# A long convolution with a gated block on Trainium2: the last phase's matmuls in plain float32 instead of high and low halves

## The chip, the cores and the metric

The kernel runs on one core of a Trainium2 chip. A core has five engines that run side by side, each through its own queue of instructions in order: TensorE (PE; its weight loads are shown as PEld), VectorE (DVE), ScalarE (ACT), GpSimd (POOL) and SyncE (SP), which here only issues transfers. Matmul results land in PSUM, everything else lies in SBUF, and transfers between SBUF and the chip's memory (DMA) are issued from SyncE's and ScalarE's queues. The metric is the time of one execution on the device in microseconds, as the median over several runs.

## The reference

All arrays are float32, with B = 4 batches, S = 12800 positions and D = 128 channels. A filter is made by a small network from a position table and multiplied with a decaying window. The product x * v is convolved causally with that filter for each channel, written with transforms of length 2S, and multiplied with x. The result goes through a gated block: a causal depthwise convolution of 5 taps and a sigmoid make the gate, a matrix makes the value, and a second matrix the output.

```python
def _attn_ref(x, v, pos_emb, w1, w2):
    h_filt = (np.maximum(pos_emb @ w1, 0.0) @ w2) * window      # [S, D]
    u = x * v
    L = 2 * S
    Uf = np.fft.rfft(u, n=L, axis=1)
    Hf = np.fft.rfft(h_filt, n=L, axis=0)
    y = np.fft.irfft(Uf * Hf[None, :, :], n=L, axis=1)[:, :S, :]
    return x * y

def _moe_ref(x, w_val, conv_w, w_out):                          # x: the result above
    gate_pre = sum(conv_w[k] * xp[:, k:k + S, :] for k in range(5))   # xp: x with 4 zeros ahead
    gate = 1.0 / (1.0 + np.exp(-gate_pre))
    return gate * (x @ w_val) @ w_out
```

## The kernel before

The sequence is cut in two blocks (index `j`) of 6400 = 100 x 64 positions, and a transform of 6400 points is done in two stages, over 100 and over 64. The kernel has three phases.

The first makes the filter and the first stage of the spectra of x * v and stores them in the chip's memory (`a_u`). The second goes over 100 frequencies: second stage, products with the filter, the inverse's first stage, stored in `c_y`. Both stay as they are, but for one thing: in the first phase the constant matrix `inv` is split in halves (L148 and L149 in the helper `split`), with the result kept for the last phase.

"Split" means that a float32 value a is written as hi + lo, both in the type float32r, where hi is a rounded to that type and lo = a - hi. A product a * b then becomes three matmuls, hi*hi, lo*hi and hi*lo, summed in PSUM.

The third phase goes over 8 units, one for each batch and block. For a unit two generators run:

- `conv_out` does the inverse's second stage and the multiplication with x. It goes over 8 chunks of 8 rows (n2), each of 100 x 2 x 1024 values from `c_y`. `prep` issues the chunk's loads two chunks ahead (x for two chunks at L431, or L434 in the last unit; c_y at L438), then makes the halves: `hi` by ScalarE (L444) and `lo` by GpSimd (L447), each in two pieces of 100 x 1024. In the first 11 chunks one of the two `lo` pieces goes to VectorE. A chunk has two groups of 4 rows. A group is six matmuls into `y_ps` (L412), a multiplication with x on VectorE (`at`, L413), four transposes on TensorE (`tp`, L394) and a copy by ScalarE into `ext` (L396), which holds the unit's result with channels on partitions.
- `gated_out` does the gated block for the unit before, in 5 pieces of 1280 positions: the gate's first tap on ScalarE (L455), four more taps on VectorE (L462, two inputs from SBUF), the sigmoid on ScalarE (L464); the value product in parts of 512, 512 and 256 columns into `v_ps`. The first part is split: `vh` on ScalarE (L489), `vl` on GpSimd (L490), three matmuls (L492); the other two parts are plain float32 (L494). VectorE multiplies with the gate (`gd`, L495), TensorE multiplies with the output matrix (`o_ps`, L506), ScalarE copies (`o_sb`, L507) and issues the store (L513).

`mix` interleaves the two generators' steps in the program's order. The first unit's `conv_out` runs alone, since no gated block is ready. The last unit is laid out by rows, and its gated block (`gated_rows`, L459 and L526 to L540) starts before its `conv_out` is done; its value products are plain float32 already. One tap of it is added by GpSimd (L459).

The order on each engine is not exactly the order of the program: a planner arranges the instructions with its own estimate of their durations before the kernel is built, keeps dependencies, and sets the waits. Buffers limit how far things run ahead: six load buffers `ld` shared by x and c_y loads (an x buffer is free after the second chunk's `at`, a c_y buffer after the last instruction that reads it), two of `y_ps`, `v_ps`, `tp3` and `o_ps` in PSUM, two of `hi`, `lo`, `vh` and `vl`. SyncE's queue holds the x and c_y loads in one order, so that a load that waits for a buffer holds up those behind it.

Of the kernel before, what the change touches and what calls it, by code (L numbers as in the profile page):

```python
# [9 lines left out]
F32 = mybir.dt.float32  # L10
F32R = mybir.dt.float32r
I32 = mybir.dt.int32
AF = mybir.ActivationFunctionType
ALU = mybir.AluOpType
PSUM = bass.MemoryType.PSUM
DRAM = bass.MemoryType.DRAM

# The causal convolution of length S = 2 * M is cut in two blocks of M = N1 * N2 samples,
# n = n1 * N2 + n2. A block's polynomial is evaluated at the M roots of z^M = i,
# k = k1 + N1 * k2, in two stages (over n1, then over n2 with the twiddles in the matrix).  # L20
# With z^M = i a product of two real blocks comes back as (low half) + i (high half), so
#   y0 = Re inv(H0 U0),   y1 = Re inv(H0 U1 + (H1 - i H0) U0)
# and no block is padded.
B, S, D, FO, KC = 4, 12800, 128, 64, 5
J, N1, N2 = 2, 100, 64
M = N1 * N2
KG = 8
P1C = 2
CH = 8
# [27 lines left out]
def _narrow(nc, pool, dst, src):  # L57
    """dst (float32) = src, whose 64-bit words are doubles, rounded to nearest."""
    p, n = dst.shape
    raw = pool.tile([p, n], mybir.dt.int64, name="raw")  # L60
    nc.scalar.dma_start(out=raw, in_=src)
    words = raw.bitcast(I32).rearrange("p (n w) -> p n w", w=2)
    lo, hi = words[:, :, 0], words[:, :, 1]
    ve = nc.vector
    top = pool.tile([p, n], I32, name="top")
    tmp = pool.tile([p, n], I32, name="tmp")
    ve.tensor_scalar(out=top, in0=hi, scalar1=0x07FFFFFF, scalar2=3, op0=ALU.bitwise_and, op1=ALU.logical_shift_left)
    ve.tensor_single_scalar(out=tmp, in_=hi, scalar=-0x40000000, op=ALU.bitwise_and)
    ve.tensor_tensor(out=top, in0=top, in1=tmp, op=ALU.bitwise_or)
    ve.tensor_single_scalar(out=tmp, in_=lo, scalar=29, op=ALU.logical_shift_right)  # L70
    ve.tensor_tensor(out=top, in0=top, in1=tmp, op=ALU.bitwise_or)
    # the 29 bits below, in units of the value's own power of two
    ve.tensor_single_scalar(out=tmp, in_=lo, scalar=0x1FFFFFFF, op=ALU.bitwise_and)
    rest = pool.tile([p, n], F32, name="rest")
    ve.tensor_copy(out=rest, in_=tmp)
    ve.tensor_single_scalar(out=tmp, in_=top, scalar=-0x00800000, op=ALU.bitwise_and)
    ve.scalar_tensor_tensor(rest, rest, 2.0 ** -52, tmp.bitcast(F32), op0=ALU.mult, op1=ALU.mult)
    ve.tensor_tensor(out=rest, in0=rest, in1=top.bitcast(F32), op=ALU.add)
    # below float32's range: zero
    ve.tensor_scalar(out=tmp, in0=hi, scalar1=27, scalar2=15, op0=ALU.logical_shift_right, op1=ALU.bitwise_and)  # L80
    keep = pool.tile([p, n], F32, name="keep")
    ve.tensor_single_scalar(out=keep, in_=tmp, scalar=7, op=ALU.is_ge)
    ve.tensor_tensor(out=dst, in0=rest, in1=keep, op=ALU.mult)
# [3 lines left out]
def tile_longconv_gate(  # L87
# [19 lines left out]
    nc = tc.nc  # L107
# [3 lines left out]

    # spectra after the first stage: [k1][re|im][n2][block][...][d]
    a_u = dram.tile([N1, 2, N2, J, B, D], F32, name="a_u")
    # products after the inverse's first stage: [block][batch][k1][re|im, n2][d]
    c_y = dram.tile([J, B, N1, 2 * N2, D], F32, name="c_y")
# [37 lines left out]

    # the filter's channels before w2, after the first stage: [re|im, n2][k1][block][channel]
    ag_pool = tc.tile_pool(name="ag", bufs=1)
    ag = ag_pool.__enter__().tile([128, N1, J, FO], F32, name="ag")

# [1 line left out]
    with tc.tile_pool(name="p1", bufs=1) as p1, tc.tile_pool(name="ps1", bufs=1, space=PSUM) as ps1:  # L159
# [4 lines left out]
        def filt():  # L164
            HC = 16
            for c0 in range(0, N2, HC):
# [3 lines left out]
                for j in range(J):  # L170
                    for n in range(0, HC, 8):
# [17 lines left out]
                        yield  # L189
            # block 1 holds H1 - i H0  # L190
            E = 4
            for j in range(J):
                for e0 in range(0, FO, E):
# [10 lines left out]
                    yield  # L204
            # the second stage, in place: [block, channel][k1][re|im, k2]
            for k0 in range(0, N1, 4):
# [35 lines left out]

        inv_split = []

        def signal():
            ready = [prep(0)]
            for i, (j, n0) in enumerate(chunks):
                if i == 8:
                    inv_split.extend(split(inv, "inv"))
                    _narrow(nc, p1, wval, w_val)  # L250
                    _narrow(nc, p1, wout, w_out)
                    _narrow(nc, p1, cw, conv_w.rearrange("k d -> d k"))
# [22 lines left out]

        # the filter's steps are spread over the signal's by their time on the tensor engine
        FS = 0.9
# [13 lines left out]

# [1 line left out]
    with tc.tile_pool(name="p2", bufs=1) as p2, tc.tile_pool(name="ps2", bufs=1, space=PSUM) as ps2:  # L293
# [3 lines left out]
        def tail(k1, g_l, z_ps, h_sb):  # L297
# [7 lines left out]

            # [V0 | H0 U1 | H1' U0], then the last two added
            v_t = p2.tile([128, J + 1, BD], F32, name="v_t2", bufs=4)
# [65 lines left out]
    ag_pool.__exit__(None, None, None)  # L373
    inv_hi, inv_lo = inv_split

# [1 line left out]
    with tc.tile_pool(name="p3", bufs=1) as p3, tc.tile_pool(name="ps3", bufs=1, space=PSUM) as ps3:  # L377
        xv = x.rearrange("b (j a n) d -> b j a n d", j=J, a=N1)
        HALO = KC - 1
        ROW_STEPS = 40  # L380
        wval_hi, wval_lo = split(wval, "wval")

        def conv_out(b, j, ext, rows=None):
            """y of one block, times x, transposed: ext[d, HALO + token]; with rows, a list
            for the chunks that are done, ext[d, HALO + n2, n1] and the last chunk first"""
            if rows is None:
# [14 lines left out]
            for q in order(b, j):  # L401
                hi, lo, xt = preps.pop(0)
                if todo:
                    preps.append(prep(*todo.pop(0)))
                at = p3.tile([N1, CH, D], F32, name="at", bufs=2)
                for g in range(CH // G):
                    y_ps = ps3.tile([N1, G, D], F32, name="y_ps", bufs=2)
                    gs = slice(g * G, (g + 1) * G)
                    es = slice(g * G * D, (g + 1) * G * D)
                    ops = [(w, d, c) for w, d in ((inv_hi, hi), (inv_lo, hi), (inv_hi, lo)) for c in range(2)]  # L410
                    for i, (w, d, c) in enumerate(ops):
                        nc.tensor.matmul(out=y_ps, lhsT=w[:, c], rhs=d[:, c, es], start=(i == 0), stop=(i == len(ops) - 1))  # L412
                    nc.vector.tensor_tensor(at[:, gs], y_ps, xt[:, gs], op=ALU.mult)  # L413
# [10 lines left out]
        def prep(b, j, q):  # L424
            ns = slice(q * CH, (q + 1) * CH)
            i = order(b, j).index(q)
            if i % 2 == 0:
# [11 lines left out]
                out=ct, in_=c_y[j, b].rearrange("k (c n) d -> k c n d", c=2)[:, :, ns].rearrange("k c n d -> k c (n d)"))  # L439
            hi = p3.tile([N1, 2, CH * D], F32R, name="hi", bufs=2)  # L440
            lo = p3.tile([N1, 2, CH * D], F32R, name="lo", bufs=2)
            for h in range(2):
                hs = slice(h * CH * D // 2, (h + 1) * CH * D // 2)
                nc.scalar.copy(out=hi[:, :, hs], in_=ct[:, :, hs])  # L444
                # until the gates run, the vector engine has room for half of this
                eng = nc.vector if h == 0 and (b * J + j) * (N2 // CH) + q < 11 else nc.gpsimd
                eng.tensor_tensor(lo[:, :, hs], ct[:, :, hs], hi[:, :, hs].bitcast(F32), op=ALU.subtract)  # L447
            return hi, lo, xt

        def gate(ext, t0, W=TCH, shift=1, pooled=0):  # L450
            """the gate's elementwise chain, an instruction at a time; pooled: taps added by GpSimd"""
            sl = lambda k: ext[:, t0 + k * shift:t0 + k * shift + W]
# [14 lines left out]
        def gated_out(b, j, ext):  # L467
# [4 lines left out]
            for t0 in range(0, M, TCH):  # L472
# [9 lines left out]
                for e in range(0, TCH, 512):  # L482
                    w = min(512, TCH - e)
                    v_ps = ps3.tile([D, 512], F32, name="v_ps", bufs=2)
                    part = ext[:, HALO + t0 + e:HALO + t0 + e + w]
                    if e == 0:
                        vh = p3.tile([D, 512], F32R, name="vh", bufs=2)
                        vl = p3.tile([D, 512], F32R, name="vl", bufs=2)
                        nc.scalar.copy(out=vh, in_=part)  # L489
                        nc.gpsimd.tensor_tensor(vl, part, vh.bitcast(F32), op=ALU.subtract)  # L490
                        for i, (a, d) in enumerate(((wval_hi, vh), (wval_lo, vh), (wval_hi, vl))):
                            nc.tensor.matmul(out=v_ps, lhsT=a, rhs=d, start=(i == 0), stop=(i == 2))  # L492
                    else:
                        nc.tensor.matmul(out=v_ps[:, :w], lhsT=wval, rhs=part, start=True, stop=True)  # L494
                    nc.vector.tensor_tensor(gd[:, e:e + w], v_ps[:, :w], sg[:, e:e + w], op=ALU.mult)  # L495
# [19 lines left out]
        def gated_rows(b, j, ext, rows):  # L515
            """the same by rows of N1 tokens, each chunk as soon as conv_out has it"""
            W = CH * N1
# [59 lines left out]

        # the last block goes by rows, so that its gate does not wait for all of it
        b, j = units[-1]
# [49 lines left out]
```

## Time and profile before

| | |
|---|---|
| median of 3 runs | 1739.79 us (1730.27 to 1749.66) |
| span of the profiled execution | 1744.1 us |
| mean granted TensorE clock | 0.887 |
| busy over the span: PE, DVE, ACT, POOL | 77%, 81%, 59%, 67% |
| share of the chain that ended last: DVE, DMA, issue, PE | 43%, 21%, 15%, 15% |
| first phase, second phase, last phase | to about 460 us, to about 1100 us, to the end |

The profile is of one execution; the span is its time from the first to the last instruction, and its share outside the span is not shown. "PEclk" is the part of TensorE's full clock that was granted. A row of instructions reads: line in the kernel, engine, operation, the tile written <- the tiles read, the shapes, xcount; then in a grouped view the busy time, the mean duration of one in nanoseconds, and the engine's idle time before them with what ended it; in the view in order of time, the row begins with its start and its length in microseconds and ends with the idle time before it in brackets. Matmul durations overlap, since matmuls are pipelined, and a matmul's cost in a stream is read from one start to the next. In the table of stretches, each engine has its busy time in that stretch and the number of instructions, and the last three columns are the granted clock, the share of the transfer engines' time and their rate.

### The profile page before, as it was taken

To read this page: it belongs to the slowest core of one execution; us is meant where nothing else is said; L and a number is where in the kernel's file an instruction comes from. 1 tells how busy PE (TensorE), PEld (TensorE's weight loads), DVE (VectorE), ACT (ScalarE), POOL (GpSimd) and SP (SyncE) were. 2 spreads that over 40 slices of the span, in tenths; PEclk is the share of its full clock that TensorE was granted. 3 is DMA by queue.
4 is the path that set the end of the run, shared out by engine and by line. 5 is a ranking of instruction groups with operands and counts; after the bars stand their busy time and mean duration, and the time that the engine had idled before them with its cause. 6 is when DMAs were issued, how large, how long until landed. Compare 5 with 4: busy or idle time off the path is not lost.

```text
span 1744.1 us, 16766 instructions
## 1 busy us (share of the span) xinstructions
PE 1344.8 (77%) x5313; PEld 873.4 (50%) x5313; DVE 1418.7 (81%) x1204; ACT 1032.3 (59%) x1657; POOL 1168.2 (67%) x528
## 2 busy tenths in 40 slices
PE   4679988767677777677777676588888888889896
PEld 3567766544323333233333232356766676667675
DVE  5663337653399999999999999269999999999996
ACT  2235446552477777677777775255656565556765
POOL 2223333333299988878888888159978697788752
PEclk9798997885799989998999999687988998888899
DMA  6666666666656656555656553565555455555512
GB/s 227 243 243 241 246 236 234 241 235 253 220 203 198 212 181 205 179 177 181 203 178 211 173 185 99 170 216 168 183 191 158 159 183 161 172 177 166 177 61 91
DMA packets 224831, 332.97 MB, mean 191 GB/s; under 512 B 7832, under 2 KB 162500, under 8 KB 220108
## 3 DMA queue, kind: packets, MB, share of 16 engines
q1 hardware_dynamic: 99358, 226.12, 38.8%
q10 hardware_dynamic: 125386, 105.79, 18.3%
q8 instruction: 43, 0.70, 0.2%
q14 instruction: 44, 0.36, 0.1%
HBM read 200.80 MB, written 131.07 MB: 190 GB/s over the span
## 4 chain that ended last, share of the span: by engine, by line
DVE 43%; DMA 21%; issue 15%; PE 15%; ACT 3%; POOL 2%; SPq 1%; ACTq 0%; POOLq 0%; DVEq 0%
DVE gt L462 16%; DMA a_u<-st 13%; DVE v_t L316 9%; DVE v_t L317 5%; PE fp L264 4%; DMA ld<-c_y 4%; DVE v_t L311 3%; DVE v_t L312 3%; DMA ld<-in_x_dram 3%; DVE at L413 2%; PE o_ps L506 2%; DVE gd L495 2%; PE y_ps L412 2%; PE z_ps L367 1%; PE c_ps L326 1%
## 5 line engine op out<-in xcount | busy, mean ns | idle before, releaser
L447 POOL TENSOR_TENSOR lo<-ld,hi 100x1024 fp32r<-100x1024 f32 x117 | 373.0, 3209 | 116.9 <-ACT hi L444 115.2
L462 DVE SCALAR_TENSOR_TENSOR gt<-ext,cw,gt 128x1280 f32<-128x1280 f32 (+1 forms) x164 | 411.5, 2521 | 10.2 <-POOL gt L459 5.3
L238 POOL TENSOR_TENSOR u_lo<-u_t,u_hi 100x1024 fp32r<-100x1024 f32 x64 | 154.2, 2411 | 302.3 <-ACT u_hi L237 263.5
L367 PE MATMUL z_ps<-ld 128*128 128x512 f32 x400 | 215.7, 666 | 117.3 <-DVE v_t L312 97.7
L311 POOL TENSOR_TENSOR q_t<-zsw,h_sb 128x1024 f32<-128x1024 f32 x100 | 241.6, 2416 | 90.2 <-ACT zsw L300 90.2
L316 DVE TENSOR_TENSOR v_t<-v_t,q_t 128x1536 f32<-128x1536 f32 x100 | 277.6, 2806 | 1.2 <-POOL q_t L312 1.2
L326 PE MATMUL c_ps<-v_t,ld 128*128 128x512 f32 x400 | 208.0, 639 | 57.2 <-POOL v_t L320 29.1
L312 POOL TENSOR_TENSOR q_t<-zsw,h_sb 128x512 f32<-128x512 f32 x100 | 225.8, 2258 | 0.0
L364 ACT COPY h_sb<-h_ps 64x256 f32<-64x256 f32 x400 | 147.1, 368 | 103.0 <-DVE v_t L312 66.7
L264 PE MATMUL fp<-u_hi,fwd_hi 100*100 100x512 f32 x256 | 127.6, 499 | 90.3 <-ACT st L267 59.3
L269 DVE COPY st<-fp 100x512 f32<-100x512 f32 x128 | 84.6, 687 | 127.9 <-DMA a_u<-st 100.0
L367 PEld LDWEIGHTS z_ps<-ld 128*128 128x128 f32 x400 | 76.6, 206 | 205.8 <-issue 166.9
L506 PEld LDWEIGHTS o_ps<-wout,gd 128*128 128x128 f32 x700 | 167.9, 320 | 11.9 <-issue 2.5
L317 DVE TENSOR_TENSOR v_t<-v_t 128x448 f32<-128x448 f32 x100 | 172.6, 1757 | 0.1
L444 ACT CAST hi<-ld 100x1024 fp32r<-100x1024 f32 x128 | 128.0, 1048 | 71.1 <-DMA ld<-c_y 44.5
L326 PEld LDWEIGHTS c_ps<-v_t,ld 128*128 128x128 f32 x400 | 77.9, 205 | 179.2 <-issue 123.3
L506 PE MATMUL o_ps<-wout,gd 128*128 128x128 f32 x700 | 164.2, 384 | 0.7 <-DVE gd L495 0.7
L299 ACT ACTIVATE zsw<-z_ps 64x1024 f32<-64x1024 f32 x100 | 102.2, 1022 | 61.1 <-PE z_ps L367 56.9
L311 DVE TENSOR_TENSOR v_t<-z_ps,h_sb 128x1024 f32<-128x1024 f32 x100 | 121.1, 1211 | 18.5 <-ACT zsw L300 18.5
L267 ACT COPY st<-fp 100x512 f32<-100x512 f32 x128 | 69.7, 591 | 110.7 <-DMA a_u<-st 85.6
L237 ACT CAST u_hi<-u_t 100x1024 fp32r<-100x1024 f32 x64 | 68.0, 1064 | 107.1 <-PE fp L264 51.6
L236 DVE TENSOR_TENSOR u_t<-ld 100x1024 f32<-100x1024 f32 x64 | 82.5, 1290 | 57.0 <-POOL u_lo L238 49.9
(93 smaller groups left out, 2696.8 us busy)
## 6 DMA issues: line engine op xcount, KB each, us to landing
c_y<-c_sb ACTq DMA_DIRECT2D x100, 512.0 KB
ld<-c_y SPq DMA_DIRECT2D x64, 800.0 KB
ld<-a_u SPq DMA_DIRECT2D x49, 1024.0 KB
ld<-in_x_dram SPq DMA_DIRECT2D x66, 400.0 KB
ld<-in_v_dram SPq DMA_DIRECT2D x64, 400.0 KB
a_u<-st ACTq DMA_DIRECT2D x64, 400.0 KB
a_u<-st SPq DMA_DIRECT2D x64, 400.0 KB
ld<-in_x_dram SPq DMA_DIRECT2D x31, 800.0 KB
```

The source lines that it names most:

```text
L238: nc.gpsimd.tensor_tensor(lo, u_t, hi.bitcast(F32), op=ALU.subtract)
L264: nc.tensor.matmul(out=fp, lhsT=w[:, c], rhs=d[:, b:b + 2], start=(k == 0), stop=(k == 2))
L311: eng.tensor_tensor(fl(t[:, 0:J]), fl(z), h_b(c, 0, J * B), op=ALU.mult)
L312: eng.tensor_tensor(fl(t[:, J:J + 1]), fl(z[:, 0:1]), h_b(c, 1, B), op=ALU.mult)
L316: nc.vector.tensor_tensor(v_t, v_t, q_t, op=ALU.add)
L317: nc.vector.tensor_tensor(v_t[:, 1, CUT:], v_t[:, 1, CUT:], v_t[:, 2, CUT:], op=ALU.add)
L326: nc.tensor.matmul(out=c_ps, lhsT=g_l, rhs=v_t[:, j], start=True, stop=True)
L364: nc.scalar.copy(out=h_sb[half * N2:(half + 1) * N2, c], in_=h_ps[c * N2:(c + 1) * N2])
L367: nc.tensor.matmul(out=z_ps[:, j], lhsT=f_l, rhs=au[:, j], start=True, stop=True)
L447: eng.tensor_tensor(lo[:, :, hs], ct[:, :, hs], hi[:, :, hs].bitcast(F32), op=ALU.subtract)
L462: nc.vector.scalar_tensor_tensor(gt, sl(k), cw[:, k:k + 1], gt, op0=ALU.mult, op1=ALU.add)
L506: nc.tensor.matmul(out=o_ps[:, i], lhsT=gv[:, g0 + i], rhs=wout, start=True, stop=True)
```

## The change

The last phase no longer uses halves. The split of `inv` in the first phase and of `wval` at the start of the last go. `prep` returns the loaded chunk `ct` itself, without `hi` and `lo`, so the loaded chunk is now read by the matmuls. A group in `conv_out` has two plain float32 matmuls into `y_ps` (one for each of the two halves, real and imaginary) instead of six split ones. The first part of the value product is one plain float32 matmul like the other two, instead of a cast, a subtraction and three split matmuls. The rest of the diff takes away comments, with the line numbers kept.

```diff
-        inv_split = []
-
         def signal():
             ready = [prep(0)]
             for i, (j, n0) in enumerate(chunks):
                 if i == 8:
-                    inv_split.extend(split(inv, "inv"))
                     _narrow(nc, p1, wval, w_val)
...
-    inv_hi, inv_lo = inv_split
...
-        wval_hi, wval_lo = split(wval, "wval")
...
             for q in order(b, j):
-                hi, lo, xt = preps.pop(0)
+                ct, xt = preps.pop(0)
...
-                    ops = [(w, d, c) for w, d in ((inv_hi, hi), (inv_lo, hi), (inv_hi, lo)) for c in range(2)]
-                    for i, (w, d, c) in enumerate(ops):
-                        nc.tensor.matmul(out=y_ps, lhsT=w[:, c], rhs=d[:, c, es], start=(i == 0), stop=(i == len(ops) - 1))
+                    for c in range(2):
+                        nc.tensor.matmul(out=y_ps, lhsT=inv[:, c], rhs=ct[:, c, es], start=(c == 0), stop=(c == 1))
                     nc.vector.tensor_tensor(at[:, gs], y_ps, xt[:, gs], op=ALU.mult)
...
-            hi = p3.tile([N1, 2, CH * D], F32R, name="hi", bufs=2)
-            lo = p3.tile([N1, 2, CH * D], F32R, name="lo", bufs=2)
-            for h in range(2):
-                hs = slice(h * CH * D // 2, (h + 1) * CH * D // 2)
-                nc.scalar.copy(out=hi[:, :, hs], in_=ct[:, :, hs])
-                eng = nc.vector if h == 0 and (b * J + j) * (N2 // CH) + q < 11 else nc.gpsimd
-                eng.tensor_tensor(lo[:, :, hs], ct[:, :, hs], hi[:, :, hs].bitcast(F32), op=ALU.subtract)
-            return hi, lo, xt
+            return ct, xt
...
-                    if e == 0:
-                        vh = p3.tile([D, 512], F32R, name="vh", bufs=2)
-                        vl = p3.tile([D, 512], F32R, name="vl", bufs=2)
-                        nc.scalar.copy(out=vh, in_=part)
-                        nc.gpsimd.tensor_tensor(vl, part, vh.bitcast(F32), op=ALU.subtract)
-                        for i, (a, d) in enumerate(((wval_hi, vh), (wval_lo, vh), (wval_hi, vl))):
-                            nc.tensor.matmul(out=v_ps, lhsT=a, rhs=d, start=(i == 0), stop=(i == 2))
-                    else:
-                        nc.tensor.matmul(out=v_ps[:, :w], lhsT=wval, rhs=part, start=True, stop=True)
+                    nc.tensor.matmul(out=v_ps[:, :w], lhsT=wval, rhs=part, start=True, stop=True)
```

## The prediction

> **What bounds the kernel now.** I read the busy shares by stretch first, cut at the last `at` multiply of each unit (a unit is one block of one batch: 8 chunks, 16 groups of four rows). The last phase starts at 1106 us. The first fence is that table for the first unit, the start of the second, one steady unit, two others and the tail, then two `at` rows that mark the cuts.
>
> ```profile
> core 0: us, PE busy (x) PEld busy (x) DVE busy (x) ACT busy (x) POOL busy (x), PEclk, DMA share, GB/s
> 1106.00:1160.00 54.00, 37.52 (x156) 24.39 (x156) 19.25 (x23) 21.83 (x30) 19.52 (x8) 0.80 0.63 211
> 1160.00:1200.00 40.00, 31.65 (x105) 20.41 (x106) 37.00 (x27) 26.94 (x35) 36.97 (x12) 0.65 0.54 176
> 1228.00:1304.00 76.00, 65.12 (x289) 52.54 (x289) 73.61 (x54) 43.86 (x61) 64.31 (x23) 0.90 0.59 186
> 1384.30:1460.60 76.30, 64.72 (x298) 52.23 (x297) 73.03 (x54) 44.85 (x63) 65.03 (x21) 0.89 0.54 172
> 1460.60:1537.10 76.50, 64.55 (x295) 52.15 (x294) 74.09 (x53) 45.40 (x63) 60.15 (x22) 0.89 0.51 164
> 1685.10:1744.10 59.00, 43.73 (x222) 34.62 (x220) 41.01 (x47) 33.93 (x48) 15.81 (x7) 0.90 0.28 89
> ...
> 1227.34 0.68 DVE L413 TENSOR_TENSOR at<-y_ps,ld 100x512 f32<-100x512 f32 x1
> 1684.46 0.68 DVE L413 TENSOR_TENSOR at<-y_ps,ld 100x512 f32<-100x512 f32 x1
> ```
>
> From 1228.0 to 1685.1 are six units: 457.1 / 6 = 76.2 us each. In each, VectorE is busy 73 to 74 us. It looks like the bound, but its instructions are stretched. The next fence gives minimum, median and maximum of three lines between 1190 and 1640 us, and the longest wait of TensorE there.
>
> ```profile
> L462 DVE SCALAR_TENSOR_TENSOR gt<-ext,cw,gt x118: 1534/2738/6090, 1190.6 to 1636.2; 128x1280 f32<-128x1280 f32 x118
> L447 POOL TENSOR_TENSOR lo<-ld,hi x97: 2353/3607/4079, 1189.2 to 1638.6; 100x1024 fp32r<-100x1024 f32 x97
> L490 POOL TENSOR_TENSOR vl<-ext,vh x30: 1271/2532/2552, 1202.3 to 1636.2; 128x512 fp32r<-128x512 f32 x30
> PE tp L394 <- DVE at L413: 47.6, 21, 5.3
> ```
>
> The same tap of the gate (L462) takes 1.53 us or 6.09 us. GpSimd's subtractions spread likewise, 2.35 to 4.08 and 1.27 to 2.55. Add the minima as if no two of these ran at once: 20 taps x 1.53 + 16 `lo` x 2.35 + 5 `vl` x 1.27 = 30.6 + 37.6 + 6.4 = 74.6 us, against a unit of 76.2. So the unit behaves as if taps and subtractions took turns on something that I call the port, and TensorE waits behind that for `at`.
>
> **The change, part by part.** (1) Removed: all 16 `lo` and 5 `vl` subtractions per unit, the `hi` and `vh` casts on ScalarE, and 11 `lo` on VectorE in the first units. VectorE's work that stays:
>
> ```profile
> L447 DVE TENSOR_TENSOR lo<-ld,hi 100x1024 fp32r<-100x1024 f32 x11 | 15.1, 1375 | 32.9 <-ACT hi L444 32.9
> L413 DVE TENSOR_TENSOR at<-y_ps,ld 100x512 f32<-100x512 f32 x128 | 85.8, 680 | 15.4 <-PE y_ps L412 15.4
> L495 DVE TENSOR_TENSOR gd<-v_ps,sg 128x512 f32<-128x512 f32 x70 | 46.8, 679 | 8.8 <-PE v_ps L494 8.2 <-ACT sg L464 0.7
> L495 DVE TENSOR_TENSOR gd<-v_ps,sg 128x256 f32<-128x256 f32 x35 | 14.4, 411 | 0.5 <-PE v_ps L494 0.5
> L444 ACT CAST hi<-ld 100x1024 fp32r<-100x1024 f32 x128 | 128.0, 1048 | 71.1 <-DMA ld<-c_y 44.5 <-PE y_ps L412 22.5 <-POOL lo L447 3.9
> L149 DVE TENSOR_TENSOR inv_lo<-inv,inv_hi 100x200 fp32r<-100x200 f32 x1 | 0.4, 368 | 0.0
> ```
>
> Per unit: 20 x 1.53 + 16 x 0.68 + 10 x 0.68 + 5 x 0.41 = 50.3 us. ScalarE loses 16 x 1.05 = 17 us of its 45, and had room anyway. Neither can bound. The splits of the two weight matrices (`inv_lo`, 0.4 us, is the longest of four such instructions) lie early in the first phase: nothing.
>
> (2) TensorE. The fence has full-clock stretches; a cost is the distance from one start to the next.
>
> ```profile
> 1396.82 1.02 PE L494 MATMUL v_ps<-ext,wval 128*128 128x512 f32 x2
> 1397.68 0.51 PE L394 MATMUL tp<-ident,at 100*128 100x100 f32 x4
> ...
> 1400.34 0.60 PE L494 MATMUL v_ps<-ext,wval 128*128 128x256 f32 x2
> 1400.78 1.42 PE L506 MATMUL o_ps<-wout,gd 128*128 128x128 f32 x6
> ...
> 1415.27 1.86 PE L506 MATMUL o_ps<-wout,gd 128*128 128x128 f32 x8
> 1416.96 0.51 PE L394 MATMUL tp<-ident,at 100*128 100x100 f32 x4
> 1417.25 0.68 PE L412 MATMUL y_ps<-hi,inv_hi 100*100 100x512 f32 x2
> ...
> 1418.68 0.95 PE L506 MATMUL o_ps<-wout,gd 128*128 128x128 f32 x4
> ...
> 1421.87 0.39 PE L492 MATMUL v_ps<-vh,wval_lo 128*128 128x512 f32 x1
> 1422.10 0.40 PE L492 MATMUL v_ps<-vl,wval_hi 128*128 128x512 f32 x1
> ```
>
> A plain float32 matmul over 512 columns is two instructions, 1397.68 - 1396.82 = 0.86 us. A split one is one instruction, 0.23 us. A `y_ps` group of six split matmuls takes 1418.68 - 1417.25 = 1.43 us; two plain ones will take 1.72 (+0.29). No row has a plain float32 matmul over 100 partitions; the split rows cost 0.23 at 100 as at 128, so I take 0.86, with 0.69 (three split ones) and twice 0.86 (the half-clock price) as far ends. The first value product goes from 3 x 0.23 = 0.69 to 0.86 (+0.17). Transposes cost 0.29 per group, eight `o_ps` instructions 1.69, the 256-column product 0.44. A unit of TensorE at full clock without waits: before, 16 x (1.43 + 0.29) + 12.5 x 1.69 + 5 x (0.69 + 0.86 + 0.44) = 27.5 + 21.1 + 10.0 = 58.6; after, 16 x (1.72 + 0.29) + 21.1 + 5 x (0.86 + 0.86 + 0.44) = 32.2 + 21.1 + 10.8 = 64.1 us. So TensorE, with 64.1 of work, becomes the bound instead of the port.
>
> How much of its 76.2 - 58.6 = 17.6 us of waits and slow clock stays? Two rows: an idle stretch with what followed, and the best stretch.
>
> ```profile
> 1409.21 0.90 PE L394 MATMUL tp<-ident,at 100*128 100x100 f32 x4 [4.04 <-DVE at L413]
> ...
> 1409.40:1416.20 6.80, 6.80 (x25) 5.61 (x25) 6.80 (x5) 4.20 (x5) 6.80 (x3) 0.62 0.59 173
> 1417.00:1427.00 10.00, 9.85 (x54) 7.66 (x53) 10.00 (x10) 9.10 (x13) 8.27 (x3) 1.00 0.55 174
> ```
>
> A wait of 4.04 us for a late `at` is followed by 6.8 us at a granted clock of 0.62; ten undisturbed microseconds run at 1.00 and 98% busy. With prompt `at`s most of it should go, though value products and `o_ps` still wait on VectorE's in-order queue (a tap ahead is 1.53 us) and the planner makes a new order. Between 64.1 / 0.985 = 65.1 and today's 76.2 I take 64.1 / 0.91 = 70.5, today's clock of about 0.9 with no more waits than that allows. Six units: 6 x (70.5 - 76.2) = -34.
>
> (3) The first two units. These rows are the last chunk of the first unit: data and cast, the end of its matmuls, the next chunk's late data, a VectorE `lo` behind that, and the delayed `at`.
>
> ```profile
> 1152.16 2.00 ACT L444 CAST hi<-ld 100x1024 fp32r<-100x1024 f32 x2 [0.94 <-DMA ld<-c_y]
> 1158.27 0.62 PE L412 MATMUL y_ps<-lo,inv_hi 100*100 100x512 f32 x2
> 1159.62 2.00 ACT L444 CAST hi<-ld 100x1024 fp32r<-100x1024 f32 x2 [3.32 <-DMA ld<-c_y]
> 1160.70 1.23 DVE L447 TENSOR_TENSOR lo<-ld,hi 100x1024 fp32r<-100x1024 f32 x1 [2.81 <-ACT hi L444]
> 1161.84 0.69 DVE L413 TENSOR_TENSOR at<-y_ps,ld 100x512 f32<-100x512 f32 x1
> ```
>
> Data is there at 1152.16; without casts its four plain matmuls, two sets of transposes and the last `at` (3.44 + 0.58 + 0.68 = 4.7 us) end near 1156.8 instead of 1162.5: -5.7. Every earlier `at` frees its x buffer sooner too, so SyncE's next loads (first the x load, then two c_y loads queued behind it) go out earlier; c_y buffers are now freed by the matmul, still before that `at`. At 211 GB/s little more comes, I put 2: -8 together. The transfers of a unit are 8 c_y loads, 4 x loads and 5 stores of these sizes:
>
> ```profile
> ld<-c_y SPq DMA_DIRECT2D x64, 800.0 KB
> ld<-in_x_dram SPq DMA_DIRECT2D x30, 800.0 KB
> out_dram<-o_sb ACTq DMA_DIRECT2D x35, 640.0 KB
> ```
>
> That is 9.8 MB of loads and 13.1 MB in all. The second unit takes 1228.0 - 1162.5 = 65.5, at a clock of 0.65 in its first 40 us; its floor is the loads at 211 GB/s, 46.6. I take 58, a little above the middle since stores and gates begin in it: -7.5. (4) The tail, 59.0 us, has only 15.8 us of GpSimd and VectorE busy for 41.0, so the port does not bound it: 0.
>
> **Sum.** Span 1744.1 - 34 - 8 - 7.5 = 1694.5. The profiled span is 4.3 us above the median shown (1739.8; runs 1730.3 to 1749.7), so 1690.
>
> **The rivals.** (A) Part goes back to waits: 9.9 us per unit of waits and slow clock stay instead of 6.4, the unit is 74, the time 1690 + 21 = 1711. For it: two `y_ps` buffers and VectorE's order. The Trainium skill, TensorE: Matmul & The Clock Gate, section on a second HAM failure mode (psum-queue depth-cycling), says that short idles between matmul groups make the clock swing. The rows show it only after a 4 us wait. (B) TensorE packs as in the best ten microseconds: 65.1 per unit, 1690 - 32 = 1658. The Trainium skill, TensorE: Matmul & The Clock Gate, section on HAM oscillation, has it that gaps under about 3.4 us leave the clock full; the trace agrees as far as the 4.04 us gap goes. (C) Transfers bind. At 172 GB/s 13.1 MB take 76 us, the unit stays, and only (3) is won: 1724. Against it: 211 GB/s in the first unit would do 62 us. (D) Slower. TensorE's waits are its own (order and PSUM buffers), all 17.6 us stay, and the dearer matmuls lie on top: the unit is 64.1 + 17.6 = 81.7, six times 5.5 = 33, and 16 x 0.29 more in each of the first two units: 1739.8 + 42 = 1782. It turns slower than before where more than 12.1 us of the 17.6 stay and (3) brings nothing. Against it: the wait row names VectorE, and the turns sum to 74.6.
>
> **Chances.** Forecast 0.54 (its own range 1672 to 1705), A 0.16, B 0.12, C 0.10, D 0.08. Faster by over 1% (below 1722; 1% is about what a measurement can tell): 0.54 + 0.16 + 0.12 = 0.82; within 1%: C, 0.10; slower: 0.08. The range runs from B to C's edge, 1658 to 1723, leaving out D and about half of B and of C.
>
> **What would show it.** Taps at 1.53 us with nearly no spread; TensorE busy over 90% of a steady unit at clock 0.9 or more; VectorE near 50 us per unit; `y_ps` groups 1.72 us; `tp <- at` waits small; units of 70 us. I am wrong if taps stay long with GpSimd idle, if `tp` still waits for `at`, or if matmuls wait for c_y loads.

## The result and the profile after

| | before | after |
|---|---|---|
| median of 4 runs each | 1744.7 us (1730.3 to 1751.3) | 1673.4 us (1670.3 to 1680.2) |
| ratio, 95% interval | | 0.961 (0.955 to 0.967) |
| span of the profiled execution | 1744.1 us | 1671.9 us |

The change takes 4% off, 71 us; 1690 was forecast, with a range of 1658 to 1723. Line numbers are lower by 3 to 22 after the change: `y_ps` is L406, `at` L407, a tap L448, `v_ps` L472, `o_ps` L484.

First the table of stretches of the changed kernel, by the same stretches as that of before: the first unit from the first c_y load, the second unit, the six steady units in one row, the tail. The next fence has the rows of the first unit and of the six steady units of the kernel before.

```profile
core 0: us, PE busy (x) PEld busy (x) DVE busy (x) ACT busy (x) POOL busy (x), PEclk, DMA share, GB/s
1115.90:1170.30 54.40, 39.86 (x124) 17.81 (x124) 11.13 (x17) 7.27 (x15) 0.00 (x0) 0.81 0.62 210
1170.30:1224.60 54.30, 49.96 (x190) 28.81 (x191) 44.82 (x47) 24.19 (x34) 0.00 (x0) 1.00 0.65 213
1224.60:1622.10 397.50, 397.16 (x1573) 270.40 (x1572) 292.32 (x321) 175.89 (x256) 6.58 (x3) 1.00 0.60 192
1622.10:1671.90 49.80, 38.91 (x211) 31.29 (x209) 33.86 (x38) 27.86 (x42) 12.98 (x6) 0.94 0.33 106
```

```profile
1102.70:1162.50 59.80, 39.21 (x161) 25.38 (x162) 21.11 (x26) 23.83 (x32) 20.27 (x9) 0.80 0.61 205
...
1228.00:1685.10 457.10, 393.19 (x1777) 316.72 (x1777) 439.52 (x316) 273.74 (x372) 371.77 (x126) 0.89 0.51 164
```

The six units take 397.5 us instead of 457.1, that is 66.2 instead of 76.2 each. TensorE is busy for 397.2 of the 397.5 us, at a granted clock of 1.00 instead of 0.89. VectorE falls from 73 to 49 us per unit, GpSimd from 62 to 1. The chain of work that ended last, within the six units, says the same: first of the kernel before (the view ends the line there), then of the changed one.

```profile
by line: DVE gt L462 55.4%; DVE at L413 8.1%; issue 8.0%; DVE gd L495 7.2%; PE y_ps L412 6.3%; PE o_ps L506 6.2%; PE v_ps L494 2.2%; PE tp L394 2.1%; PE v_ps L492 1.4%; ACT gt L455 1.2%; DVE ext L571 0.6%; ACT ext L396 0.4%; DVE ext L585 0.
```

```profile
by line: PE y_ps L406 38.9%; PE o_ps L484 33.5%; PE v_ps L472 16.0%; PE tp L389 7.9%; DVE gt L448 2.2%; DVE at L407 0.6%; DVE gd L473 0.6%; issue 0.4%
```

It went over taps, and goes over TensorE's four kinds of matmul. The next fence is from the changed kernel: minimum, median and maximum of the taps in those units (six of 800 columns, of the last unit, are among the 126), TensorE's wait for `at`, and TensorE in order of time.

```profile
L448 DVE SCALAR_TENSOR_TENSOR gt<-ext,cw,gt x126: 1042/1543/1552, 1233.4 to 1622.0; 128x1280 f32<-128x1280 f32 x120, 128x800 f32<-128x800 f32 x6
...
PE tp L389 <- DVE at L407: 0.3, 2, 0.2
...
1424.75 1.88 PE L406 MATMUL y_ps<-ld,inv 100*100 100x512 f32 x4
1426.46 0.51 PE L389 MATMUL tp<-ident,at 100*128 100x100 f32 x4
1426.81 1.02 PE L406 MATMUL y_ps<-ld,inv 100*100 100x512 f32 x2
```

A tap of 1280 columns now takes 1.54 us and at most 1.55, where it took 1.53 to 6.09. A `y_ps` group costs 1426.46 - 1424.75 = 1.71 us, and TensorE waited for an `at` for 0.3 us in all, where 47.6 were shown before.

By stretch of the two profiled executions, in us:

| stretch | before | after | difference | forecast |
|---|---|---|---|---|
| up to the first c_y load | 1102.7 | 1115.9 | +13.2 | 0 |
| first unit | 59.8 | 54.4 | -5.4 | -8 |
| second unit | 65.5 | 54.3 | -11.2 | -7.5 |
| six units | 457.1 | 397.5 | -59.6 | -34 |
| tail | 59.0 | 49.8 | -9.2 | 0 |
| span | 1744.1 | 1671.9 | -72.2 | -49.5 |

### The profile page after: what moved, and what is told of

Read it like the earlier page. It is cut to its first block, busy times and chain, and to the rows that moved or that the text cites. A ratio compares the mean times of both kernels' runs of the same rounds, so it can differ in the third digit from the quotient of the medians.

```text
span 1671.9 us, 15690 instructions
## 1 busy us (share of the span) xinstructions
PE 1338.8 (80%) x5022; PEld 804.8 (48%) x5022; DVE 1228.0 (73%) x1189; ACT 891.3 (53%) x1494; POOL 718.0 (43%) x376
## 4 chain that ended last, share of the span: by engine, by line
PE 34%; DVE 25%; DMA 23%; issue 13%; ACT 2%; POOL 1%; SPq 1%; ACTq 0%; DVEq 0%; POOLq 0%
DMA a_u<-st 14%; PE y_ps L406 12%; DVE v_t L313 10%; PE o_ps L484 9%; DVE v_t L314 5%; DMA ld<-in_v_dram 5%; PE v_ps L472 4%; DVE v_t L308 4%; PE fp L261 3%; DVE v_t L309 3%; PE tp L389 2%; DMA ld<-c_y 2%; DVE gt L448 2%; PE z_ps L364 1%; DMA ld<-in_x_dram 1%
## 5 line engine op out<-in xcount | busy, mean ns | idle before, releaser
L313 DVE TENSOR_TENSOR v_t<-v_t,q_t 128x1536 f32<-128x1536 f32 x100 | 274.1, 2770 | 1.2 <-POOL q_t L309 1.2
L406 PE MATMUL y_ps<-ld,inv 100*100 100x512 f32 x512 | 248.4, 606 | 20.2 <-DMA ld<-c_y 20.2
L448 DVE SCALAR_TENSOR_TENSOR gt<-ext,cw,gt 128x1280 f32<-128x1280 f32 (+1 forms) x164 | 243.6, 1502 | 9.3 <-ACT gt L441 6.3
L323 PE MATMUL c_ps<-v_t,ld 128*128 128x512 f32 x400 | 204.1, 629 | 54.4 <-POOL v_t L317 32.8
L445 POOL TENSOR_TENSOR gt<-gt,g 128x800 f32<-128x800 f32 x8 | 19.6, 2445 | 529.3 <-ACT gt L441 525.8
L484 PEld LDWEIGHTS o_ps<-wout,gd 128*128 128x128 f32 x700 | 169.7, 318 | 24.4 <-issue 12.3
L484 PE MATMUL o_ps<-wout,gd 128*128 128x128 f32 x700 | 163.0, 378 | 0.0
L407 DVE TENSOR_TENSOR at<-y_ps,ld 100x512 f32<-100x512 f32 x128 | 87.9, 688 | 101.6 <-PE y_ps L406 101.4
L485 ACT COPY o_sb<-o_ps 128x512 f32<-128x512 f32 (+1 forms) x105 | 54.0, 514 | 164.2 <-PE o_ps L484 164.1
L391 ACT COPY ext<-tp 128x400 f32<-128x400 f32 x128 | 68.5, 539 | 134.9 <-PE tp L389 132.4
```

Source lines behind the costliest of these rows:

```text
L313: nc.vector.tensor_tensor(v_t, v_t, q_t, op=ALU.add)
L323: nc.tensor.matmul(out=c_ps, lhsT=g_l, rhs=v_t[:, j], start=True, stop=True)
L406: nc.tensor.matmul(out=y_ps, lhsT=inv[:, c], rhs=ct[:, c, es], start=(c == 0), stop=(c == 1))
L448: nc.vector.scalar_tensor_tensor(gt, sl(k), cw[:, k:k + 1], gt, op0=ALU.mult, op1=ALU.add)
L484: nc.tensor.matmul(out=o_ps[:, i], lhsT=gv[:, g0 + i], rhs=wout, start=True, stop=True)
```

## The experiments

Two theories were set against each other. The port theory: the gate's taps on VectorE and GpSimd's subtractions take turns, and their sum paced the unit before; with them gone TensorE's own work paces it. The chain theory: a matmul that no longer waits for load, cast and subtraction is what helped.

**One half of the change at a time.** `y_only` leaves the value product in halves, `v_only` the inverse's second stage.

```diff
 y_only, against the changed kernel:
+        wval_hi, wval_lo = split(wval, "wval")
...
-                    nc.tensor.matmul(out=v_ps[:, :w], lhsT=wval, rhs=part, start=True, stop=True)
+                    if e == 0:
+                        vh = p3.tile([D, 512], F32R, name="vh", bufs=2)
+                        vl = p3.tile([D, 512], F32R, name="vl", bufs=2)
+                        nc.scalar.copy(out=vh, in_=part)
+                        nc.gpsimd.tensor_tensor(vl, part, vh.bitcast(F32), op=ALU.subtract)
...
+                    else:
+                        nc.tensor.matmul(out=v_ps[:, :w], lhsT=wval, rhs=part, start=True, stop=True)
 v_only, against the kernel before:
-        wval_hi, wval_lo = split(wval, "wval")
...
-                    if e == 0:
...
-                    else:
-                        nc.tensor.matmul(out=v_ps[:, :w], lhsT=wval, rhs=part, start=True, stop=True)
+                    nc.tensor.matmul(out=v_ps[:, :w], lhsT=wval, rhs=part, start=True, stop=True)
```

> Only the inverse's second stage is plain float32; the value product keeps its halves. Port theory (taps of the gate and GpSimd's subtractions take turns): per steady unit 30.6 us of taps and 6.4 of vl, 37 in all, far below TensorE's 63.2, so TensorE stays the bound and the time is 1665 to 1685, taps near 1.54 us at the median with a few of 2 to 3 us. Chain theory (what helped is that a matmul no longer waits for load, cast and subtraction): 1670 to 1680 too, with no stretched taps. Rival that the value product's halves matter most: 1720 or more.

> Only the value product is plain float32; the inverse's second stage keeps its halves. Port theory: taps 30.6 and lo 37.6 us per steady unit, 68.2 together instead of 74.6, so a unit falls from 76.2 to about 70 and the time from 1745 to about 1705 (1690 to 1720), taps still stretched to 2.5 us or so. Chain theory: the chain load, cast, subtraction, matmul of the inverse is untouched, so 1735 to 1750.

Measured: `y_only` 1670.3 us (ratio to before 0.959, 0.955 to 0.963), not to be told from the whole change, as both theories had it. `v_only` 1712.4 us (0.983, 0.979 to 0.987), in the port theory's range and outside the chain theory's. The fence has its taps and its six steady units.

```profile
L461 DVE SCALAR_TENSOR_TENSOR gt<-ext,cw,gt x120: 1532/2462/3733, 1228.5 to 1651.5; 128x1280 f32<-128x1280 f32 x120
...
1228.60:1651.50 422.90, 383.00 (x1729) 302.31 (x1727) 391.83 (x313) 254.54 (x340) 291.28 (x95) 0.91 0.55 177
```

Six units in 422.9 us are 70.5 each, where 68.2 of taps and subtractions were counted. With the chain of the inverse untouched, 5.7 us per unit went together with 6.4 us of `vl`. But the value product's own chain of cast, subtraction and matmul went with it, so this run alone does not decide between the theories; the next two do.

**GpSimd's work put back, with nobody waiting for it.** `pool_back` subtracts the loaded chunk from itself, `pool_at` the finished `at` tile.

```diff
 pool_back:
+            lo = p3.tile([N1, 2, CH * D], F32R, name="lo", bufs=2)
+            for h in range(2):
+                hs = slice(h * CH * D // 2, (h + 1) * CH * D // 2)
+                nc.gpsimd.tensor_tensor(lo[:, :, hs], ct[:, :, hs], ct[:, :, hs], op=ALU.subtract)
             return ct, xt
...
+                    if e == 0:
+                        vl = p3.tile([D, 512], F32R, name="vl", bufs=2)
+                        nc.gpsimd.tensor_tensor(vl, part, part, op=ALU.subtract)
 pool_at (and bufs=4 for at):
                     nc.vector.tensor_tensor(at[:, gs], y_ps, xt[:, gs], op=ALU.mult)
+                    if g == 1:
+                        for h in range(2):
+                            lo = p3.tile([N1, CH, D], F32R, name="lo", bufs=2)
+                            nc.gpsimd.tensor_tensor(lo, at, at, op=ALU.subtract)
```

> The changed kernel, to which GpSimd's subtractions are added again (16 of 100x1024 and 5 of 128x512 per unit, same sizes and types); no other instruction reads what they write, though they hold the loaded chunk. Port theory: 74.6 us per unit on the port again, units of 75 to 80 us, time 1730 to 1765, taps stretched to 2.7 us, TensorE waiting for at again with dips of the clock. Chain theory: nobody waits for the subtractions, so 1670 to 1685.

> The changed kernel with 16 subtractions of 100x1024 per unit added on GpSimd; they read the finished at tile (four buffers) instead of the loaded chunk, and no other instruction reads what they write. Port theory: taps 30.6 and subtractions 37.6 us take turns, 68.2 per unit, so units of 69 to 72 and 1695 to 1715, taps stretched to 2 us or more. Rival that pool_back lost its time by holding the loaded chunk and waiting for transfers: 1670 to 1685, units 66 to 67, whatever the taps take.

Measured: `pool_back` 1732.0 us (0.993, 0.990 to 0.995), `pool_at` 1702.0 us (0.977, 0.972 to 0.982), both times in the port theory's ranges. Of `pool_at` the taps, first by minimum, median and maximum, then in the grouped view, and the six units:

```profile
L452 DVE SCALAR_TENSOR_TENSOR gt<-ext,cw,gt x123: 1034/1551/3258, 1237.3 to 1639.3; 128x1280 f32<-128x1280 f32 x120, 128x800 f32<-128x800 f32 x3
...
L452 DVE SCALAR_TENSOR_TENSOR gt<-ext,cw,gt 128x1280 f32<-128x1280 f32 x120 | 243.9, 2049 | 6.2 <-ACT gt L445 6.2
...
1228.50:1645.60 417.10, 403.53 (x1571) 271.08 (x1569) 350.76 (x318) 174.58 (x254) 277.39 (x99) 0.98 0.57 182
```

The taps are stretched again, to 3.26 us at most, though the median stays at 1.55; "2 us or more" holds for the mean alone (2.05). The unit is 417.1 / 6 = 69.5 us beside 68.2 counted. `pool_back` reached 442.8 / 6 = 73.8 beside 74.6:

```profile
1239.80:1682.60 442.80, 414.66 (x1573) 274.66 (x1572) 376.45 (x321) 176.28 (x255) 307.89 (x125) 0.97 0.54 171
```

The 75 to 80 us per unit that were expected of `pool_back` were a miss. That work nobody reads costs 29 us (1702.0 - 1673.4) and more is what the chain theory cannot explain. Nor did it cost that by holding buffers: in `pool_at` no `at` waited for a subtraction longer than 1.1 us, 2.3 us in all.

How the two take turns can be seen in single instructions of `pool_at`. In the first pair a tap was running when the subtraction started: three taps in a row kept their 1.5 us each, and the subtraction took 5.99. In the second pair the subtraction kept its 1.89 us, and the tap took 3.26:

```profile
1306.29 4.47 DVE L452 SCALAR_TENSOR_TENSOR gt<-ext,cw,gt 128x1280 f32<-128x1280 f32 x3
1306.52 5.99 POOL L411 TENSOR_TENSOR lo<-at 100x1024 fp32r<-100x1024 f32 x1 [2.23 <-DVE at L407]
...
1312.45 3.26 DVE L452 SCALAR_TENSOR_TENSOR gt<-ext,cw,gt 128x1280 f32<-128x1280 f32 x1
1312.47 1.89 POOL L411 TENSOR_TENSOR lo<-at 100x1024 fp32r<-100x1024 f32 x1
```

That the sum of the minima sets the period is not shown, though. The subtractions that were put back are shorter than those of the kernel before (2.35 and 1.27 us), whose minima the counts of 68.2 and 74.6 use. These are the rows of `pool_at`, then of `pool_back`:

```profile
L411 POOL TENSOR_TENSOR lo<-at x97: 1882/3069/5993, 1227.0 to 1642.0; 100x1024 fp32r<-100x1024 f32 x97
...
L437 POOL TENSOR_TENSOR lo<-ld x93: 1886/3091/5760, 1239.6 to 1660.9; 100x1024 fp32r<-100x1024 f32 x93
L478 POOL TENSOR_TENSOR vl<-ext x30: 1032/2282/2288, 1250.4 to 1630.5; 128x512 fp32r<-128x512 f32 x30
```

With their own minima the counts are 30.6 + 16 x 1.88 = 60.7 us for `pool_at`, less than TensorE's 64.1, and 30.6 + 16 x 1.89 + 5 x 1.03 = 66.0 for `pool_back`, beside 69.5 and 73.8 measured. Nor was the port ever full: going by the start and end of each instruction, a tap or an instruction of GpSimd ran for 70.0 of 76.2 us per unit in the kernel before, 63.9 of 70.5 in `v_only`, 58.8 of 69.5 in `pool_at` and 62.1 of 73.8 in `pool_back`. So it was partly luck that the times of `pool_at` and `pool_back` fell in their ranges. What is shown is that the two block each other, that VectorE's instructions get longer by it, and that TensorE then waits: in `pool_at` 12.4 us for `at` over the six units, at a clock of 0.98.

**ScalarE's casts put back.** `act_back` casts the loaded chunk, `act_at` the finished `at`; nobody reads the casts.

```diff
 act_back:
+            hi = p3.tile([N1, 2, CH * D], F32R, name="hi", bufs=2)
+            for h in range(2):
+                hs = slice(h * CH * D // 2, (h + 1) * CH * D // 2)
+                nc.scalar.copy(out=hi[:, :, hs], in_=ct[:, :, hs])
             return ct, xt
 act_at (and bufs=4 for at):
+                    if g == 1:
+                        for h in range(2):
+                            hi = p3.tile([N1, CH, D], F32R, name="hi", bufs=2)
+                            nc.scalar.copy(out=hi, in_=at)
```

> The changed kernel, to which the casts of the loaded chunk on ScalarE are added again (16 of 100x1024 per unit, 17 us); no other instruction reads them. Port theory: ScalarE goes from 28 to 45 us of a 66 us unit and stays off the path: 1670 to 1685. Rival that ScalarE's load was part of it: 1690 or more.

> The changed kernel with 16 casts of 100x1024 per unit added on ScalarE, as in act_back, but they read the finished at tile (which gets four buffers) instead of the chunk that is still being loaded; no other instruction reads what they write. Queue theory (in act_back the casts stood in ScalarE's in-order queue waiting for transfers, 113.7 us between 1250 and 1600 us, with the copies of ext and o_sb behind them): 1670 to 1685, units 66 to 67. Load theory (45 us of ScalarE work per unit is too much by itself): 1705 to 1720, units about 71.

`act_back` was a miss for the port theory: 1715.7 us (0.983, 0.977 to 0.990), 71.0 us per unit, with taps of 1.55 us at most and GpSimd idle. Its longest waits in the six units, except for GpSimd's one wait for the last unit:

```profile
ACT hi L437 <- DMA ld<-c_y: 124.5, 44, 5.6
PEld y_ps L406 <- issue: 51.2, 186, 0.6
DVE gt L452 <- ACT gt L445: 46.9, 15, 7.4
```

44 times a cast came up before its chunk was there, and in ScalarE's queue the first tap of the gate and the copies stood behind it, so that VectorE waited 46.9 us for ScalarE. Transfers of c_y make up 44% of the chain that ended last in these units. `act_at` has as many casts of the same size, of data that is there: 1675.8 us (0.962, 0.956 to 0.967), the changed kernel's time. So the casts' work is free in a unit of 66 us, and their place in an in-order queue behind a transfer is not. In the kernel before this cost nothing in the six units: none of ScalarE's waits there is for a transfer. So `act_back` says what casts would cost in the faster units of the changed kernel, not what the change won.

**Is TensorE the bound now?** `half` leaves out the second matmul of each `y_ps` group.

```diff
-                    for c in range(2):
-                        nc.tensor.matmul(out=y_ps, lhsT=inv[:, c], rhs=ct[:, c, es], start=(c == 0), stop=(c == 1))
+                    nc.tensor.matmul(out=y_ps, lhsT=inv[:, 0], rhs=ct[:, 0, es], start=True, stop=True)
```

> The changed kernel without the second matmul of each y_ps group (the imaginary half is loaded but not used). TensorE theory (after the change TensorE's 64.1 us of work per unit is the bound): its work falls to 50.3, the unit falls to the next bound, 13.1 MB of transfers at about 215 GB/s or 61 us, VectorE at 48; 1635 to 1660. Rival that order and buffers pace the unit: units stay near 66 and the time at 1670 to 1675.

Measured: 1593.2 us (0.916, 0.910 to 0.921), below the range. The six units:

```profile
1206.10:1521.20 315.10, 311.44 (x1355) 232.43 (x1354) 285.17 (x314) 169.10 (x246) 0.00 (x0) 1.00 0.66 240
```

315.1 / 6 = 52.5 us per unit beside TensorE's 50.3 counted, with TensorE busy for 311.4. TensorE paces the unit even there. The transfers, which I took to bind at 61 us, moved 240 GB/s: the 211 to 215 GB/s of the first units were no limit of theirs.

**A better version.** `y_v2` keeps the inverse plain and takes both 512-column value parts in halves, since three split matmuls (0.69 us) are cheaper than a plain one (0.86) and GpSimd is idle.

```diff
 against y_only:
-                    if e == 0:
+                    if w == 512:
                         vh = p3.tile([D, 512], F32R, name="vh", bufs=2)
```

> A version that may beat both: the inverse's second stage plain, both 512-column parts of the value product in halves (three matmuls of 0.23 us instead of 0.86). TensorE theory: 64.1 - 10 x 0.17 = 62.4 us per unit, 7 x 1.7 = 12 us less than the changed kernel: 1655 to 1668; taps and vl together 43 us, so the port does not bind. Rival that the casts and subtractions cost the path as much as the matmuls save: 1670 or more.

Measured: 1664.1 us (0.955, 0.950 to 0.959), as expected: 63.8 us per unit beside 62.4 counted and 66.2 of the changed kernel.

**The first phase.** Up to the first c_y load the changed kernel was 13 us slower, with the same order of instructions there but for the dropped splits and two VectorE copies that changed places with a neighbour. Three kernels and a second profile of the kernel before look at that.

```diff
 inv_kept, against the changed kernel; y_v2_inv, against y_v2:
                 if i == 8:
+                    split(inv, "inv")
 pad, against the changed kernel:
+    pad = const.tile([128, 656], F32, name="pad")
...
+    nc.gpsimd.memset(pad, 0.0)
```

> The changed kernel, in which the split of inv stays in the first phase though nothing uses it. The first c_y load went out at 1102.7 and 1104.0 us in the two profiles whose first phase splits inv, and at 1110.6 to 1119.4 in the eight without it. Theory that the dropped split (its instructions or the room of its tiles) slows the first phase by some 12 us: first c_y load at 1100 to 1107, time 1658 to 1666. Rival that this is chance between executions: 1110 to 1119 and 1670 to 1677.

> The changed kernel with an unused constant tile of 2624 bytes per partition, the room of the four dropped constant tiles, set once by GpSimd at the start; the order of the other engines is that of the changed kernel. If the place of the load buffers in SBUF is what slows the first phase: first c_y load at 1100 to 1107, time 1658 to 1666. If it is the missing split instructions, or chance: 1110 to 1119, 1670 to 1677.

> y_v2 (inverse plain, both 512-column value parts in halves) with the unused split of inv kept in the first phase. If the dropped split costs some 12 us: 1664 - 12 = 1652 (1646 to 1658), first c_y load at 1100 to 1107. If not: 1660 to 1668.

> The kernel before again, for a second profile. If the early first c_y load belongs to its first phase: 1100 to 1107 us. If it is chance between executions: anywhere from 1100 to 1120.

| kernel | median of the runs | ratio to before | first c_y load |
|---|---|---|---|
| changed kernel | 1673.4 us | 0.961 | 1115.9 us |
| `inv_kept` | 1663.1 us | 0.954 (0.951 to 0.958) | 1101.9 us |
| `pad` | 1666.8 us | 0.955 (0.952 to 0.958) | 1102.2 us |
| `y_v2` | 1664.1 us | 0.955 (0.950 to 0.959) | 1112.4 us |
| `y_v2_inv` | 1654.2 us | 0.949 (0.945 to 0.953) | 1104.7 us |
| `ctl_before` | 1751.3 us (one run) | | 1110.1 us |

Two rows of the transfers in the first 450 us, of the changed kernel and of `pad`, show where it comes from:

```profile
0.00:450.00 450.00, 340.85 (x1856) 250.59 (x1856) 219.00 (x351) 187.28 (x332) 142.54 (x63) 0.85 0.67 231
```

```profile
0.00:450.00 450.00, 348.43 (x1891) 254.46 (x1892) 231.60 (x360) 195.79 (x342) 151.61 (x67) 0.83 0.66 237
```

At the same share of the transfer engines' time the changed kernel moved 231 GB/s and `pad` 237. Over all profiles, the first c_y load went out at 1101.9 to 1110.1 us in the six profiles with the room of the `inv` halves (of the kernel before, `v_only`, `inv_kept`, `pad`, `y_v2_inv` and `ctl_before`), and at 1110.6 to 1119.4 in the eight without; the rates are 235 to 239 GB/s and 231 to 235. An unused tile is enough, so it is rather where things lie in SBUF than the instructions. But two profiles of the same kernel, before and `ctl_before`, are 7.4 us apart, so that `ctl_before` fell where its expectation had put chance; the 95% intervals of the ratios overlap in each pair; the runs of `pad` (1657 to 1670) touch those of the changed kernel (1670 to 1680); and `pad` missed its expected time by 1 us. Some 7 to 10 us in the medians speak for it three times; the cause is not shown, and which address matters, and why, stays open. `y_v2_inv` has the lowest median of the versions that compute the whole result, 5.1% below the kernel before.

## Why the prediction was right, and where its sizes were off

What bounds the kernel: right in the mechanism, taps and subtractions blocked each other, as `pool_at` and `pool_back` show. The sum that led there, 74.6 us of minima against a unit of 76.2, agreed better than it should have: a tap or a GpSimd instruction ran for only 70.0 us of the unit, so the two overlapped in part, and for 6 us neither ran. What filled the unit was VectorE with its stretched taps, busy for 439.5 of the 457.1 us. The Trainium skill, SBUF — State Buffer, section on who interferes with whom, states the cause: VectorE with two SBUF inputs needs a read interface that GpSimd's reads use, and the ports that the two share are an exclusive lock. The trace agrees: the taps (two inputs from SBUF) stretch from 1.53 to 6.09 us, in the pairs of `pool_at` above one keeps its time and the other waits, and `at`, which has one input in PSUM, kept its time in the kernel before:

```profile
L413 DVE TENSOR_TENSOR at<-y_ps,ld x94: 674/678/693, 1196.5 to 1638.8; 100x512 f32<-100x512 f32 x94
```

(1) What is removed: right in size. VectorE is busy 49 us per unit (50.3 forecast). That ScalarE "had room anyway" was argued from its busy time only; `act_back` shows that this misses what a queue does to the instructions behind it, though in the six units of the kernel before it did no harm.

(2) TensorE's work: right. A group costs 1.71 us (1.72), and `half` takes 52.5 where 50.3 was counted, so TensorE is the new bound.

The step that was mis-sized is the one after it: "Between 64.1 / 0.985 = 65.1 and today's 76.2 I take 64.1 / 0.91 = 70.5, today's clock of about 0.9". The unit was 66.2. Of the 17.6 us of waits and slow clock nothing to speak of stayed, where 6.4 was put: TensorE was busy for 397.2 of 397.5 us, and the clock was granted in full (1.00) once no `at` was late. The 2.1 us above 64.1 are work that the count left out. The transposes of a group took 1426.81 - 1426.46 = 0.35 us ahead of a plain matmul instead of 0.29, about 1 us per unit, and the stretch held a little more than six units of gated work (620 `o_ps` instructions instead of 600), about 1 us more. So 70.5 was 4.3 us too long, six times that is the 26 us by which the unit term was off, and it is rival (B) that came near in the steady units (65.1); (A), which left 9.9 us of waits and slow clock, did not.

The Trainium skill, TensorE: Matmul & The Clock Gate, section on HAM oscillation, ties the slow clock to idle gaps of more than about 3.4 us. The clock of 1.00 with 0.3 us of waiting agrees, but other runs do not bear the threshold out, and so the prediction's reading that the clock swings only after a 4 us wait is too narrow. In `v_only` the clock was 0.91, and no matmul waited longer than 3.2 us; in `act_back` it was 0.98, with none above 2.0 us. A wait and the slow stretch with it, first of `v_only`, then of `act_back`:

```profile
1325.17 0.90 PE L393 MATMUL tp<-ident,at 100*128 100x100 f32 x4 [3.13 <-DVE at L412]
1323.30:1330.10 6.80, 4.93 (x17) 3.75 (x18) 4.95 (x7) 6.14 (x7) 4.72 (x2) 0.50 0.63 227
...
1283.79 1.28 PE L488 MATMUL o_ps<-wout,gd 128*128 128x128 f32 x4 [1.97 <-ACT o_sb L489]
1284.70:1288.10 3.40, 3.40 (x10) 1.71 (x10) 0.88 (x1) 3.11 (x4) 0.00 (x0) 0.50 0.64 211
```

So a halved clock also goes with short waits, as (A) had it; in the changed kernel hardly any wait was left.

(3) The first two units: -16.6 measured for -15.5, but divided otherwise (-5.4 and -11.2). (4) The tail gave 9.2 us where none was forecast. Its work had in part moved ahead: after the last `at` 18 taps were left instead of 24. Over all profiles the tail goes by the number of taps left (49.7 to 49.9 us with 18, 51.9 to 57.0 with 21, 57.1 and 59.0 with 24, 59.8 with 25, 60.2 with 27), so it is the planner's order that moves it. The first phase gave 13.2 back, which the prediction set at nothing on the ground that four short instructions went; the runs put 7 to 10 of that on the room that the tiles left, not with certainty.

Rival (C) fell: the steady units moved 192 GB/s, and transfers reached 240 in `half`. Rival (D) fell: TensorE's waits were VectorE's lateness, and went with it.

The time of 1673.4 lies 17 us below the forecast. In the span it is 23 us (1694.5 to 1671.9): 26 from the steady units, 9 from the tail and 1 from the first two units, against 13 not foreseen in the first phase. The other 6 go the other way: the median of the runs lies 1.5 us above the profiled span after the change, where 4.3 below was carried over. That the time lies within the forecast's own range, 1672 to 1705, is luck: without the 13.2 us lost ahead of the third phase it would have been about 1660, next to (B).

## What to carry to other kernels

When an instruction's median is far above its minimum, look for an engine whose instructions stretch beside it. A sum of minima near the period is a hint and no proof; here it came out close for partly wrong reasons, and only putting the work back with nobody reading it settled the cause. Taking one of the two engines off paid here although it made TensorE's work dearer, 64.1 us instead of 58.6. Compare that third engine's work at full clock, not at today's mean clock, since the slow clock went here with the very waits that went. And an idle engine's work is free only where its place in the queue is: a cast that waits for a transfer holds all that stands behind it.

## What the runs showed of the hardware that was not expected

The tiny copies of four columns per partition, SBUF to SBUF on VectorE, show the same taking of turns far more strongly than the taps. One row of the kernel before, one of the changed kernel, grouped by line:

```profile
L571 DVE COPY ext<-ext 128x4 f32<-128x4 f32 x3 | 4.5, 1510 | 0.0
```

```profile
L549 DVE COPY ext<-ext 128x4 f32<-128x4 f32 x3 | 0.5, 162 | 0.2 <-ACT ext L391 0.2
```

Beside a busy GpSimd one took 1.51 us in the mean, beside an idle one 0.16. One of the three, and the subtraction that was running when it started:

```profile
1165.92 1.75 DVE L571 COPY ext<-ext 128x4 f32<-128x4 f32 x1
1165.22 2.42 POOL L447 TENSOR_TENSOR lo<-ld,hi 100x1024 fp32r<-100x1024 f32 x1 [1.06 <-ACT hi L444]
```

The copy ended at 1165.92 + 1.75 = 1167.67 us, the subtraction at 1165.22 + 2.42 = 1167.64: the copy waited for its end. The Trainium skill, SBUF — State Buffer, section on who interferes with whom, names copies among the instructions that can take the shared pair; no run here shows by which mode these did. And TensorE's clock was granted in full through 397.5 us without a break (1.00), where its mean had been 0.89.
